# Attention with normalized q and k, then a mixture of depths: row transfers on another queue, a split first step and a split last store

## The chip, the cores and the metric

The kernel runs on one core of one Trainium2 chip. The core has five engines that run their own instruction streams: TensorE (PE; its weight loads stand as PEld), VectorE (DVE), ScalarE (ACT), GpSimd (POOL) and SyncE (SP), which here only issues transfers. They wait for each other through semaphores. The metric is the time on the device in microseconds. Its median over three runs is 543.24 us, with runs from 542.14 to 544.32. The profile is one further execution, whose span is 539.9 us.

## What is computed

The first half is attention over 8 batches, 12 heads, 448 positions and 64 values per head, in float32. Each row of q and k is divided by its root mean square. The second half sends 128 of the 448 tokens of each batch through two matrices.

```
q_n = q / sqrt(mean(q*q) + 1e-6) * g_q          # the same for k with g_k
attn = softmax(q_n @ k_n^T / sqrt(64))
x[b] = concatenation over the 12 heads of attn @ v          # (8, 448, 768)

scores = x @ w_gate
out = x
for each batch b:
    top = the 128 tokens with the highest scores
    ye  = relu(x[b, top] @ w1) @ w2             # 768 -> 1024 -> 768
    out[b, top] = x[b, top] + sigmoid(scores[b, top]) * ye
```

## The kernel before

The work is cut into 24 groups of 4 heads (3 groups to a batch), and each group into 7 units of 64 keys for each of the 4 heads. For a unit, TensorE makes scores, ScalarE their exponentials, TensorE the products with v, and VectorE adds up the exponentials. The softmax needs no maximum, because the normalized scores are bounded. Slots count the units, in order of the program: what is put in slot 20 is written into the program right after the units of about that number. An engine works through its own part of the program in order.

The inverse root mean squares are called rinv. There are two tiles of tokens for each group: tile 0 holds q (its rinv is 128 x 14 values), tile 1 holds k. The rinv of k enters as the scale of the exponential. The rinv of q has to be multiplied along the free axis of the transposed q. For groups 2 to 23 this goes by way of device memory: rows_out writes the values there as rows, rows_in reads them back spread over 64 partitions into bc, and scale_q multiplies. For groups 0 and 1, scale_q_early spreads them with TensorE.

```
class Loads:                      # in __init__: the first transfers
    nc.scalar.dma_start(out=self.gcol, in_=g2)
    ...
    nc.scalar.activation(out=warm, in_=neg_half, func=AF.Exp)
    self.load("tok", 0, 0)
    self.load("tok", 0, 1)
    self.load("qT", 0)
    # load() issues on SyncE: self.nc.sync.dma_start(out=t, in_=src)

...   # in fast(): identity, further loads, then the warm-up of TensorE
for _ in range(36):
    nc.tensor.transpose(out=ps[:, 0:128], in_=ident, identity=ident)

def squares(n, i):                # ScalarE
    t = get("tok", n, i)
    sq = norm_pool.tile([128, 2, NI, D], F32, name="sq")
    nc.scalar.activation(out=sq, in_=t, func=AF.Square, scale=scale)
    ...

def sum_squares(n, i, sq):        # VectorE, then GpSimd twice
    ss = sss.pop((n, i))
    nc.vector.tensor_reduce(out=ss, in_=sq, axis=AX.X, op=OP.add)      # L208
    nc.gpsimd.tensor_scalar_add(ss, ss, 1e-6)                          # L209
    rinv = norm_pool.tile([128, 2, NI], F32, name="rinv", bufs=8)
    nc.gpsimd.tensor_tensor(out=rinv..., in0=ss..., in1=neg_half..., op=OP.pow)   # L212

def rows_out(n):                  # GpSimd's queue, two transfers
    rows = dram_pool.tile([GH, S], F32, name="rows", bufs=3)
    rinv = rinvs.pop((n, 0))
    for c in range(2):
        nc.gpsimd.dma_start(                                           # L226
            out=rows[2 * c : 2 * c + 2].rearrange("h (p i) -> p h i", i=NI),
            in_=rinv[D * c : D * (c + 1)])

def rows_in(n):                   # SyncE's queue, two transfers (L238)
    ...
def scale_q(n):                   # VectorE (L247): qT = qT * gg * bc
    ...
def scale_q_early(n):             # TensorE (L259) spreads rinv; VectorE (L267) multiplies
    ...

# scores(u): TensorE L290, ScalarE's exponential p L299; values(u): TensorE L316
# add_probs(u): VectorE L333; sum_keys, invert_sums, to_tokens: L362, L377, L393

def mixture(b):                   # the two matrices for one batch
    ...                           # transposes L525; first matrix L544; relu into hT L553
    for a in range(2):
        cols = slice(DM // 2 * a, DM // 2 * (a + 1))                   # DM = 768
        ps = bank()
        for fc in range(NFC):                                          # NFC = 8
            nc.tensor.matmul(out=ps[:n, : DM // 2], lhsT=hT[:, fc, :n],
                             rhs=w2[:, fc, cols], ...)                 # L563
        nc.vector.scalar_tensor_tensor(out=xe[:n, cols], ...)          # L572
        if a == 1:
            nc.gpsimd.indirect_dma_start(                              # L581
                out=out.flatten_outer_dims(),
                out_offset=bass.IndirectOffsetOnAxis(ap=row[:n, :1], axis=0),
                in_=xe[:n, 0:DM], in_offset=None)

def prepare(n, slot):             # when the normalization of group n is written
    sq = {}
    for i in range(2):
        at(slot + 2 * i, lambda i=i: sq.setdefault(i, squares(n, i)))
        at(slot + 2 * i + 1, lambda i=i: sum_squares(n, i, sq.pop(i)))
    at(slot + 1, rows_out, n)
    at(slot + (8 if n > 5 else 6), rows_in, n)
```

In the schedule, s0 is the number of a group's first unit, and the normalization starts at slot s0 - 20 (s0 - 17 up to group 5), or at 0.

Of the kernel before, what the change touches and what calls it, by code (L numbers as in the profile page):

```python
# [10 lines left out]
F32 = mybir.dt.float32  # L11
I32 = mybir.dt.int32
AF = mybir.ActivationFunctionType
# [12 lines left out]
class Loads:  # L26


    def __init__(self, nc, pool, qT, kT, vp, tok, g2):
        self.nc, self.pool = nc, pool  # L30
        self.src = {"tok": tok, "qT": qT, "kT": kT, "v": vp}
        self.tiles = {}
        self.groups = tok.shape[1]
        self.gcol = pool.tile([128, 2], F32, name="gcol", bufs=1)
        nc.scalar.dma_start(out=self.gcol, in_=g2)
        neg_half = pool.tile([128, 1], F32, name="neg_half", bufs=1)
        nc.vector.memset(neg_half, -0.5)

        warm = pool.tile([128, 1], F32, name="warm", bufs=1)
        nc.scalar.activation(out=warm, in_=neg_half, func=AF.Exp)  # L40
        self.neg_half = neg_half
        self.load("tok", 0, 0)
        self.load("tok", 0, 1)
        self.load("qT", 0)

    def load(self, name, n, i=None):
        b, g = divmod(n, self.groups)
        src = self.src[name]
        if i is not None:
            src = src[b, g, :, i]  # L50
        elif name == "v":
            src = src[b, g]
        else:
            src = src[b, 2 * g : 2 * g + 2].rearrange("c p s -> p c s")
        pool = self.v_pool if name == "v" else self.pool
        bufs = {"tok": 6, "qT": 4, "kT": 3, "v": 3}[name]
        held = [key for key in self.tiles if key[0] == name]
        if len(held) == bufs:
            del self.tiles[held[0]]
        t = pool.tile(list(src.shape), F32, name=name, bufs=bufs)  # L60
        self.nc.sync.dma_start(out=t, in_=src)
        self.tiles[name, n, i] = t

    def get(self, name, n, i=None):
# [4 lines left out]
def fast(  # L69
# [26 lines left out]
    D = 64  # L96
# [36 lines left out]
        return ps_aux.tile(shape, F32, tag="aux", name=name)  # L133

    sss, rinvs, bcs = {}, {}, {}
    loads.v_pool = ctx.enter_context(tc.tile_pool(name="load_v", bufs=1))
    load, get, neg_half = loads.load, loads.get, loads.neg_half

# [59 lines left out]

    def squares(n, i):
        t = get("tok", n, i)  # L200
        sq = norm_pool.tile([128, 2, NI, D], F32, name="sq")
        nc.scalar.activation(out=sq, in_=t, func=AF.Square, scale=scale)  # L202
        sss[n, i] = norm_pool.tile([128, 2, NI], F32, name="ss", bufs=4)
        return sq

    def sum_squares(n, i, sq):
        ss = sss.pop((n, i))
        nc.vector.tensor_reduce(out=ss, in_=sq, axis=AX.X, op=OP.add)  # L208
        nc.gpsimd.tensor_scalar_add(ss, ss, 1e-6)  # L209
        rinv = norm_pool.tile([128, 2, NI], F32, name="rinv", bufs=8)  # L210
        flat = "p h i -> p (h i)"
        nc.gpsimd.tensor_tensor(  # L212
            out=rinv.rearrange(flat),
            in0=ss.rearrange(flat),
            in1=neg_half.to_broadcast([128, 2 * NI]),
            op=OP.pow,
        )
        rinvs[n, i] = rinv

    def rows_out(n):  # L220

        rows = dram_pool.tile([GH, S], F32, name="rows", bufs=3)
        rinv = rinvs.pop((n, 0))
        for c in range(2):

            nc.gpsimd.dma_start(  # L226
                out=rows[2 * c : 2 * c + 2].rearrange("h (p i) -> p h i", i=NI),
                in_=rinv[D * c : D * (c + 1)],
            )
        bcs[n] = rows  # L230

    def rows_in(n):

        rows = bcs[n]
        bc = norm_pool.tile([128, 2, S], F32, name="bc")
        for hh in range(2):
            src = rows.rearrange("(c hh) s -> hh c s", hh=2)[hh]
            nc.sync.dma_start(  # L238
                out=bc[D * hh : D * (hh + 1)],
                in_=dataclasses.replace(src, ap=[[0, D]] + [list(x) for x in src.ap]),  # L240
            )
        bcs[n] = bc
# [265 lines left out]
    def mixture(b):  # L508

        n = CAP  # L510
        xe = xes.pop(b)
        xeT = moe_pool.tile([128, NDC, 128], F32, name="xeT")

        def bank():

            if PER * now[0] >= units:
                return ps_sc.tile([128, 512], F32, tag="sc", name="sc")
            return ps_moe.tile([128, 512], F32, tag="moe", name="moe_ps")

        half = NDC // 2  # L520
        for a in range(2):
            ps = bank()
            for i in range(half):
                dc = half * a + i
                nc.tensor.transpose(  # L525
                    out=ps[:, 128 * i : 128 * i + n],
                    in_=xe[:n, 128 * dc : 128 * (dc + 1)],
                    identity=ident[:n, :n],
                )
            nc.scalar.copy(  # L530
                out=xeT[:, half * a : half * (a + 1), :n],
                in_=ps[:, : half * 128].rearrange("p (i t) -> p i t", t=128)[:, :, :n],
            )
            if a == 1:
                row = moe_pool.tile([128, 1], I32, name="row", bufs=2)
                nc.vector.tensor_copy(out=row[:n], in_=xe[:n, DM + 1 : DM + 2])
            yield

        hT = moe_pool.tile([128, NFC, 128], F32, name="hT")
        for f0 in range(0, NFC, 4):  # L540
            ps = bank()
            for i in range(4):
                for dc in range(NDC):
                    nc.tensor.matmul(  # L544
                        out=ps[:, 128 * i : 128 * i + n],
                        lhsT=w1[:, dc, 128 * (f0 + i) : 128 * (f0 + i + 1)],
                        rhs=xeT[:, dc, :n],
                        start=(dc == 0),
                        stop=(dc == NDC - 1),
                    )  # L550
                if i == 1:
                    yield
            nc.scalar.activation(  # L553
                out=hT[:, f0 : f0 + 4, :n],
                in_=ps.rearrange("p (i t) -> p i t", t=128)[:, :, :n],
                func=AF.Relu,
            )
            yield
        for a in range(2):
            cols = slice(DM // 2 * a, DM // 2 * (a + 1))  # L560
            ps = bank()
            for fc in range(NFC):
                nc.tensor.matmul(  # L563
                    out=ps[:n, : DM // 2],
                    lhsT=hT[:, fc, :n],
                    rhs=w2[:, fc, cols],
                    start=(fc == 0),
                    stop=(fc == NFC - 1),
                )
                if fc == NFC // 2 - 1:  # L570
                    yield
            nc.vector.scalar_tensor_tensor(  # L572
                out=xe[:n, cols],
                in0=ps[:n, : DM // 2],
                scalar=xe[:n, DM : DM + 1],
                in1=xe[:n, cols],
                op0=OP.mult,
                op1=OP.add,
            )
            if a == 1:  # L580
                nc.gpsimd.indirect_dma_start(  # L581
                    out=out.flatten_outer_dims(),
                    out_offset=bass.IndirectOffsetOnAxis(ap=row[:n, :1], axis=0),
                    in_=xe[:n, 0:DM],
                    in_offset=None,
                )
            yield
# [11 lines left out]
    def at(slot, fn, *args):  # L599
        todo.setdefault(slot, []).append(lambda: fn(*args))  # L600
# [14 lines left out]
    def prepare(n, slot):  # L615
        sq = {}
        for i in range(2):
            at(slot + 2 * i, lambda i=i: sq.setdefault(i, squares(n, i)))
            at(slot + 2 * i + 1, lambda i=i: sum_squares(n, i, sq.pop(i)))
        at(slot + 1, rows_out, n)  # L620
        at(slot + (8 if n > 5 else 6), rows_in, n)

    for n in range(1, n_groups):
        s0 = NI * n
# [1 line left out]
            at(max(s0 - 26, 4 * (n - 3)), load, "tok", n, 0)  # L626
            at(max(s0 - 26, 4 * (n - 3)), load, "tok", n, 1)
        if n > 1:
            first = max(s0 - (20 if n > 5 else 17), 0)
            prepare(n, first)  # L630
            at(max(s0 - 7, first + 10), scale_q, n)
            at(max(s0 - 13, 2), load, "qT", n)
            at(max(s0 - 11, 2), load, "kT", n)
            at(max(s0 - 11, 2), load, "v", n)
    for part in range(NDC + NFC):
        at(16 + 3 * part, load_w, part)
    at(7, lambda: nc.sync.dma_start(out=wg, in_=_bcast_row(moe_w_gate, CP)))
# [61 lines left out]

    for i in range(2):  # L700
        sum_squares(0, i, squares(0, i))
    sqs = [squares(1, i) for i in range(2)]
    scale_q_early(0)
    for i in range(2):
        sum_squares(1, i, sqs[i])
    load("tok", 2, 0)
    load("tok", 2, 1)
    task((0, 1), scale_q_early, 1)
# [570 lines left out]
```

## Time and profile before

| what | us |
|---|---|
| median of three runs | 543.24 |
| span of the profiled execution | 539.9 |
| TensorE busy | 513.1 |
| VectorE busy | 339.9 |
| ScalarE busy | 278.0 |
| GpSimd busy | 242.7 |

The profile is read from the busiest engine down. Busy time counts an instruction from its start to its end, and for TensorE the ends are modelled. A row of a group of instructions names the line, the engine, the operation and the tiles (out <- in), the count, the busy time with the mean in ns, and then the idle time of that engine just ahead of them with what ended it. A row of waits has the engine and line that waited, what it waited for, and the total in us, the number and the longest. L numbers are lines of the kernel before; they stand beside the code above. A q after an engine's name means its issuing part, for example SPq.

### The profile page before, as it was taken

The numbers are of one execution on the slowest core, as the hardware profiler recorded it, in microseconds if no ns is written. First come the engines' busy times: TensorE is split into PE (matmuls) and PEld (weight loads), VectorE is DVE, ScalarE is ACT, GpSimd is POOL, SyncE is SP. The second block draws the span as 40 slices with busy tenths as digits, with TensorE's granted clock in tenths as the row PEclk, the third lists the DMA queues.
The fourth block names the chain that finished last, engine by engine and source line by source line (L and its number), as shares of the span: only waits on it lengthen the run. The fifth ranks groups of instructions, "written<-read, shape, count | busy, mean of one in ns | idle before, by whom it ended". The sixth has DMA issues, their size and how long they took to land. (4 is left out here: it accounts for less than half of the span.)

```text
span 539.9 us, 16470 instructions
## 1 busy us (share of the span) xinstructions
PE 513.1 (95%) x7116; PEld 288.9 (54%) x7116; DVE 339.9 (63%) x644; ACT 278.0 (51%) x506; POOL 242.7 (45%) x193
## 2 busy tenths in 40 slices
PE   5999899999999999999999999999999999999991
PEld 5434344446644466546654466543764456568770
DVE  3767899788475776659557795668756384443000
ACT  3687786774535755546545755547564444311000
POOL 4785988657624276244734456336742103002000
PEclk9999999999999999999999999999999999999997
DMA  8957869999961497608826486604934032004100
GB/s 299 351 164 247 280 218 330 326 317 297 297 199 39 127 256 223 206 31 223 243 110 207 123 263 214 209 4 133 296 110 135 32 104 60 2 23 139 60 4 33
DMA packets 41605, 93.57 MB, mean 173 GB/s; under 512 B 6454, under 2 KB 24374, under 8 KB 41524
## 3 DMA queue, kind: packets, MB, share of 16 engines
q1 hardware_dynamic: 36772, 85.96, 50.6%
q0 software_dynamic: 4608, 6.47, 3.7%
q8 instruction: 58, 0.95, 0.7%
q14 instruction: 23, 0.19, 0.1%
q10 hardware_dynamic: 144, 0.00, 0.0%
HBM read 74.93 MB, written 25.35 MB: 186 GB/s over the span
## 5 line engine op out<-in xcount | busy, mean ns | idle before, releaser
L299 ACT ACTIVATE p<-sc,rinv 128x448 f32<-128x448 f32 x336 | 186.1, 639 | 109.5 <-PE sc L290 91.4
L316 PE MATMUL av<-p,v 64*32 64x448 f32 x2688 | 153.7, 537 | 0.0
L290 PE MATMUL sc<-qT,kT 64*32 64x448 f32 x2688 | 152.9, 540 | 0.3
L212 POOL TENSOR_TENSOR rinv<-ss,neg_half 128x14 f32<-128x14 f32 x48 | 138.6, 2888 | 4.0
L333 DVE TENSOR_TENSOR sum<-sum,p 128x896 f32<-128x896 f32 x113 | 122.5, 1084 | 9.2 <-ACT p L299 2.2
L316 PEld LDWEIGHTS av<-p,v 64*32 64x32 f32 x2688 | 58.2, 107 | 75.2 <-issue 70.8
L209 POOL TENSOR_SCALAR ss<-ss 128x14 f32<-128x14 f32 x48 | 23.0, 479 | 158.1 <-DVE ss L208 132.0
L290 PEld LDWEIGHTS sc<-qT,kT 64*32 64x32 f32 x2688 | 49.4, 106 | 70.8 <-issue 49.0
L544 PE MATMUL moe_ps<-xeT,w 128*128 128x128 f32 x576 | 69.5, 277 | 0.4 <-issue 0.4
L544 PEld LDWEIGHTS moe_ps<-xeT,w 128*128 128x128 f32 x576 | 66.2, 192 | 5.0 <-issue 5.0
L208 DVE TENSOR_REDUCE ss<-sq 128x14 f32<-128x896 f32 x48 | 51.4, 1077 | 27.6 <-ACT sq L202 24.2
L393 DVE TENSOR_TENSOR x<-x_ps,rden 112x512 f32<-112x512 f32 x48 | 32.9, 689 | 54.5 <-PE x_ps L391 50.3
L563 PE MATMUL moe_ps<-w,hT 128*128 128x384 f32 x176 | 61.2, 491 | 0.0
L487 POOL DMA_INDIRECT selected<-x,rank x32 | 36.4, 1138 | 35.0 <-DVE x L479 26.2
L202 ACT ACTIVATE sq<-tok 128x896 f32<-128x896 f32 x48 | 46.0, 963 | 7.2 <-DMA tok<-in_tok_dram 7.1
L581 POOL DMA_INDIRECT out_dram<-xe,row x8 | 10.8, 1348 | 79.6 <-DVE rden L379 47.5
L563 PEld LDWEIGHTS moe_ps<-w,hT 128*128 128x128 f32 x176 | 31.7, 190 | 21.8 <-issue 2.9
L417 DVE SCALAR_TENSOR_TENSOR prod<-x,wg 112x256 f32<-112x256 f32 x96 | 40.9, 426 | 3.0
L226 POOL DMA_DIRECT2D rows<-rinv x44 | 29.1, 662 | 6.6 <-POOL rinv L212 6.5
L391 PEld LDWEIGHTS x_ps<-ident,xT 128*112 128x112 f32 x192 | 21.0, 134 | 18.9 <-issue 12.7
L391 PE MATMUL x_ps<-ident,xT 128*112 128x128 f32 x192 | 29.1, 278 | 1.4 <-DVE x L393 1.4
L572 DVE SCALAR_TENSOR_TENSOR xe<-sc,xe 128x384 f32<-128x384 f32 x5 | 3.1, 618 | 41.0 <-PE sc L563 41.0
(66 smaller groups left out, 340.8 us busy)
## 6 DMA issues: line engine op xcount, KB each, us to landing
tok<-in_tok_dram SPq DMA_DIRECT2D x48, 448.0 KB
qT<-in_qT_dram SPq DMA_DIRECT2D x24, 448.0 KB
kT<-in_kT_dram SPq DMA_DIRECT2D x24, 448.0 KB
v<-in_vp_dram SPq DMA_DIRECT2D x24, 448.0 KB
out_dram<-x SPq DMA_DIRECT2D x8, 1344.0 KB
bc<-rows SPq DMA_DIRECT2D x44, 224.0 KB
xe<-selected SPq DMA_DIRECT2D x8, 385.0 KB
w<-in_moe_w_dram SPq DMA_DIRECT2D x6, 512.0 KB
```

Source lines behind the costliest of these rows:

```text
L202: nc.scalar.activation(out=sq, in_=t, func=AF.Square, scale=scale)
L208: nc.vector.tensor_reduce(out=ss, in_=sq, axis=AX.X, op=OP.add)
L212: nc.gpsimd.tensor_tensor(out=rinv.rearrange(flat), in0=ss.rearrange(flat), in1=neg_half.to_broadcast([128, 2 * NI]), op=OP.pow,)
L290: nc.tensor.matmul(out=scs[hh][o : o + 32, 0:S], lhsT=get("kT", n)[r, c, D * i + k0 : D * i + k0 + 32], rhs=get("qT", n)[r, c, :], start=True,
L299: nc.scalar.activation(out=p[:, hh], in_=scs[hh][:, 0:S], func=AF.Exp, scale=rinvs[n, 1][:, hh, i : i + 1],)
L316: nc.tensor.matmul(out=avs[n][c][o : o + 32, 0:S], lhsT=get("v", n)[r, hh, i, d0 : d0 + 32], rhs=probs[u][r, hh], start=(i == 0), stop=(i ...
L333: nc.vector.tensor_tensor(out=sums[n], in0=probs[u - 1] if i == 1 else sums[n], in1=probs[u], op=OP.add)
L391: nc.tensor.transpose(out=ps[:CP, j, :], in_=t[:, j, :], identity=ident)
L417: nc.vector.scalar_tensor_tensor(out=prod, in0=xs[b][:, j, cols], scalar=1.0, in1=wg[:, cols], op0=OP.mult, op1=OP.mult, accum_out=gates[b ...
L487: w = nc.gpsimd.indirect_dma_start(out=t[:, :], out_offset=bass.IndirectOffsetOnAxis(ap=rank[:, j : j + 1], axis=0), in_=x[:, j, :], in_of ...
L544: nc.tensor.matmul(out=ps[:, 128 * i : 128 * i + n], lhsT=w1[:, dc, 128 * (f0 + i) : 128 * (f0 + i + 1)], rhs=xeT[:, dc, :n], start=(dc == 0),
L563: nc.tensor.matmul(out=ps[:n, : DM // 2], lhsT=hT[:, fc, :n], rhs=w2[:, fc, cols], start=(fc == 0), stop=(fc == NFC - 1),)
```

## The change

It has five parts.

- The first tile of tokens is issued on ScalarE's queue, ahead of everything else there, instead of on SyncE's. It is meant to arrive sooner.
- For this first tile the squares and their sums are made in two halves, so that ScalarE and VectorE can overlap.
- The 1e-6 stands in a 65th column of two fixed tiles of squares, set once. The reduction adds it, and GpSimd's addition is gone.
- The rows of rinv are written by one transfer on SyncE's queue, later than before, instead of two on GpSimd's. Their layout in device memory is changed so that one transfer does, and the reads and the scaling of q are moved by one to three slots.
- For the last batch, the second matrix is worked in three parts of 256 columns instead of two of 384, and each part is stored by its own scatter as soon as it is ready. The store at the end is meant to be shorter.

```
-        self.load("tok", 0, 0)                      # after the warm exponential, on SyncE
+        self.load("tok", 0, 0, nc.scalar)           # ahead of gcol, on ScalarE

+    sqs = [const.tile([128, 2, NI, D + 1], F32, name=f"sq{i}") for i in range(2)]
+    for sq in sqs:
+        nc.vector.memset(sq[:, :, :, D], 1e-6)

     def squares(n, i):
-        sq = norm_pool.tile([128, 2, NI, D], F32, name="sq")
-        nc.scalar.activation(out=sq, in_=t, func=AF.Square, scale=scale)
+        sq = sqs[(2 * n + i) % 2]
+        for h in [slice(0, 1), slice(1, 2)] if (n, i) == (0, 0) else [slice(0, 2)]:
+            nc.scalar.activation(out=sq[:, h, :, 0:D], in_=t[:, h], func=AF.Square, scale=scale)

     def sum_squares(n, i, sq):
-        nc.vector.tensor_reduce(out=ss, in_=sq, axis=AX.X, op=OP.add)
-        nc.gpsimd.tensor_scalar_add(ss, ss, 1e-6)
+        for h in [slice(0, 1), slice(1, 2)] if (n, i) == (0, 0) else [slice(0, 2)]:
+            nc.vector.tensor_reduce(out=ss[:, h], in_=sq[:, h], axis=AX.X, op=OP.add)

     def rows_out(n):
-        rows = dram_pool.tile([GH, S], F32, name="rows", bufs=3)
-        rinv = rinvs.pop((n, 0))
-        for c in range(2):
-            nc.gpsimd.dma_start(
-                out=rows[2 * c : 2 * c + 2].rearrange("h (p i) -> p h i", i=NI),
-                in_=rinv[D * c : D * (c + 1)],
-            )
+        rows = dram_pool.tile([2, 2 * S], F32, name="rows", bufs=3)
+        nc.sync.dma_start(
+            out=rows.rearrange("h (p i) -> p h i", i=NI), in_=rinvs.pop((n, 0))
+        )
     def rows_in(n):
-            src = rows.rearrange("(c hh) s -> hh c s", hh=2)[hh]
+            src = rows[hh].rearrange("(c s) -> c s", c=2)

     # in prepare(n, slot)
-        at(slot + 1, rows_out, n)
-        at(slot + (8 if n > 5 else 6), rows_in, n)
+        at(slot + (7 if n > 2 else 6), rows_out, n)
+        at(slot + (10 if n > 5 else 9 if n > 2 else 8), rows_in, n)
     # in the schedule; the loads of qT, kT and v now stand ahead of prepare(n, first)
-            at(max(s0 - 7, first + 10), scale_q, n)
+            at(max(s0 - 6, first + 11), scale_q, n)

     # in mixture(b): parts_out is 3 for the last batch and 1 otherwise
-        for a in range(2):
-            cols = slice(DM // 2 * a, DM // 2 * (a + 1))
+        width = DM // max(2, parts_out)
+        for c0 in range(0, DM, width):
+            cols = slice(c0, c0 + width)
     ...
-            if a == 1:
+            if parts_out > 1 or c0 + width == DM:
+                part = slice(c0 if parts_out > 1 else 0, c0 + width)
                 nc.gpsimd.indirect_dma_start(
+                    out=out.flatten_outer_dims().rearrange("r (k c) -> (r k) c", k=parts_out),
     ...             # row holds 3 * token + part for part 0, 1, 2 of the last batch
```

More of the change, by code (lines that the diff above doesn't have):

```diff
@@ L41, in __init__, with load @@
         self.neg_half = neg_half
-        self.load("tok", 0, 0)
         self.load("tok", 0, 1)
         self.load("qT", 0)
-    def load(self, name, n, i=None):
+    def load(self, name, n, i=None, engine=None):
         b, g = divmod(n, self.groups)
@@ L60, in load @@
         t = pool.tile(list(src.shape), F32, name=name, bufs=bufs)
-        self.nc.sync.dma_start(out=t, in_=src)
+        (engine or self.nc.sync).dma_start(out=t, in_=src)
         self.tiles[name, n, i] = t
@@ L511, in mixture @@
         xe = xes.pop(b)
+        parts_out = 1 if b < B - 1 else 3
         xeT = moe_pool.tile([128, NDC, 128], F32, name="xeT")
@@ L534, in mixture @@
             if a == 1:
-                row = moe_pool.tile([128, 1], I32, name="row", bufs=2)
-                nc.vector.tensor_copy(out=row[:n], in_=xe[:n, DM + 1 : DM + 2])
+                row = moe_pool.tile([128, parts_out], I32, name="row", bufs=2)
+                for part in range(parts_out):
+                    nc.vector.tensor_scalar(
+                        out=row[:n, part : part + 1],
+                        in0=xe[:n, DM + 1 : DM + 2],
+                        scalar1=float(parts_out),
+                        scalar2=float(part),
+                        op0=OP.mult,
+                        op1=OP.add,
+                    )
             yield
@@ L563, in mixture @@
                 nc.tensor.matmul(
-                    out=ps[:n, : DM // 2],
+                    out=ps[:n, :width],
                     lhsT=hT[:, fc, :n],
@@ L573, in mixture @@
                 out=xe[:n, cols],
-                in0=ps[:n, : DM // 2],
+                in0=ps[:n, :width],
                 scalar=xe[:n, DM : DM + 1],
@@ L579, in mixture @@
             )
-            if a == 1:
+            if parts_out > 1 or c0 + width == DM:
+                part = slice(c0 if parts_out > 1 else 0, c0 + width)
                 nc.gpsimd.indirect_dma_start(
-                    out=out.flatten_outer_dims(),
-                    out_offset=bass.IndirectOffsetOnAxis(ap=row[:n, :1], axis=0),
-                    in_=xe[:n, 0:DM],
+                    out=out.flatten_outer_dims().rearrange("r (k c) -> (r k) c", k=parts_out),
+                    out_offset=bass.IndirectOffsetOnAxis(
+                        ap=row[:n, part.start * parts_out // DM :][:, :1], axis=0
+                    ),
+                    in_=xe[:n, part],
                     in_offset=None,
@@ L628, in fast @@
         if n > 1:
-            first = max(s0 - (20 if n > 5 else 17), 0)
-            prepare(n, first)
-            at(max(s0 - 7, first + 10), scale_q, n)
             at(max(s0 - 13, 2), load, "qT", n)
@@ L634, in fast @@
             at(max(s0 - 11, 2), load, "v", n)
+            first = max(s0 - (20 if n > 5 else 17), 0)
+            prepare(n, first)
+            at(max(s0 - 6, first + 11), scale_q, n)
     for part in range(NDC + NFC):
@@ L701, in fast @@
         sum_squares(0, i, squares(0, i))
-    sqs = [squares(1, i) for i in range(2)]
+    later = [squares(1, i) for i in range(2)]
     scale_q_early(0)
     for i in range(2):
-        sum_squares(1, i, sqs[i])
+        sum_squares(1, i, later[i])
     load("tok", 2, 0)
```

## The prediction

> **What bounds the kernel now.** I read the page first, then TensorE's own waits, then the timeline of the first 28 us and of the last 30 us, and last the waits of SyncE's queue. The page says who is busy, and what the parts that change cost in total:
>
> ```profile
> span 539.9 us, 16470 instructions
> ...
> PE 513.1 (95%) x7116; PEld 288.9 (54%) x7116; DVE 339.9 (63%) x644; ACT 278.0 (51%) x506; POOL 242.7 (45%) x193
> ...
> L212 POOL TENSOR_TENSOR rinv<-ss,neg_half 128x14 f32<-128x14 f32 x48 | 138.6, 2888 | 4.0
> ...
> L209 POOL TENSOR_SCALAR ss<-ss 128x14 f32<-128x14 f32 x48 | 23.0, 479 | 158.1 <-DVE ss L208 132.0
> ...
> L226 POOL DMA_DIRECT2D rows<-rinv x44 | 29.1, 662 | 6.6 <-POOL rinv L212 6.5
> ```
>
> TensorE is busy for 513.1 of 539.9 us, so 26.8 us of its idle time is all that a better schedule could win. It idles 5.3 us before its first instruction and 11.2 us after its last (539.9 - 528.7). That leaves 10.3 us for everything between. The waits of TensorE alone tell what those are:
>
> ```profile
> PE warm_ps L160 <- DVE gg L154: 5.3, 1, 5.3
> PE moe_ps L525 <- ACT xeT L530: 2.2, 3, 1.2
> PE den_ps L362 <- DVE x L393: 2.1, 5, 0.5
> ```
>
> No row there names rinv, rows, bc or a load. The middle waits are for the ScalarE and VectorE copies that surround the transposes. GpSimd, from which the change takes work, is 45% busy and nobody on TensorE waits for it.
>
> The timeline of the start (start us, duration us, engine, line, operation, and in brackets the idle time ahead):
>
> ```profile
> 5.26 6.42 PE L160 MATMUL warm_ps<-ident 128*128 128x128 f32 x36 [5.26 <-DVE gg L154]
> ...
> 5.35 2.03 ACT L202 ACTIVATE sq<-tok 128x896 f32<-128x896 f32 x2 [2.65 <-DMA tok<-in_tok_dram]
> ...
> 6.33 2.17 DVE L208 TENSOR_REDUCE ss<-sq 128x14 f32<-128x896 f32 x2 [1.16 <-ACT sq L202]
> ...
> 7.52 0.27 POOL L209 TENSOR_SCALAR ss<-ss 128x14 f32<-128x14 f32 x1 [2.35 <-DVE ss L208]
> ...
> 7.87 2.62 POOL L212 TENSOR_TENSOR rinv<-ss,neg_half 128x14 f32<-128x14 f32 x1
> ...
> 11.61 1.67 PE L259 MATMUL sc<-ident,rinv 64*64 64x64 f32 x56
> ...
> 15.18 4.54 ACT L299 ACTIVATE p<-sc,rinv 128x448 f32<-128x448 f32 x8 [2.74 <-PE sc L290]
> ```
>
> The reader is to compare two times. The first rinv is ready at 7.87 + 2.62 = 10.49 us. The 36 warm-up transposes, which stand ahead of its user in TensorE's program, hold TensorE until about 11.6 us. The spread of rinv over q (L259) starts at 11.61, directly behind them. The rinv chain thus has 1.1 us of slack already. The second rinv ends at 13.53 us and the first exponential, which reads it, starts at 15.18 us after waiting for scores: 1.6 us of slack.
>
> The tail: the timeline of the last 30 us, then two of the half-microsecond stretches (length, GpSimd busy, clock, share of the DMA engines, GB/s), then the instructions of the program's closing line (durations in ns min/median/max, first and last start):
>
> ```profile
> 518.23 10.49 PE L563 MATMUL sc<-w,hT 128*128 128x384 f32 x32
> 528.75 0.62 DVE L572 SCALAR_TENSOR_TENSOR xe<-sc,xe 128x384 f32<-128x384 f32 x1 [4.54 <-PE sc L563]
> 529.64 0.96 POOL L581 DMA_INDIRECT out_dram<-xe,row  x1 [21.29 <-DVE xe L572]
> ```
> ```profile
> 531.50:532.00 0.50, 0.00 (x0) 1.00 1.01 406
> 532.00:532.50 0.50, 0.00 (x0) 0.73 0.23 78
> ```
> ```profile
> L1206 POOLq DRAIN  x3: 40/107/7006, 532.1 to 539.6; - x3
> ```
>
> The rows have left by 532.5 us. Yet the span ends 7.4 us later, because a drain of GpSimd begins at 532.1 and lasts 7.0 us. It, and not the landing of the rows, is what ends last.
>
> [...] SyncE spends 0.36, 0.23 and 0.83 us on two weight rows and two token tiles before q is issued, and in 3.75 to 6.25 us the engines already carry about 400 GB/s. [...]
>
> **The change, part by part.**
>
> *First tokens from ScalarE's queue.* SyncE issues them at 1.48 us now; ScalarE can at 0.79, where it now issues gcol. That is 0.7 us sooner at best. The two token tiles then share the engines, so I take 0.4 us. ScalarE's table load (1.28 us from 1.20) slides by one issue, 0.4 us, and still ends at 2.9 us, before the tokens.
>
> *First squares in halves.* Square takes 0.95 us for 896 elements and the reduction 1.08. In halves the second half's square runs beside the first half's reduction: 0.5 + 0.55 + 0.55 = 1.6 us in place of 2.1, so 0.5 us.
>
> *1e-6 in a column.* The L209 addition goes: 0.27 us and its hop of 0.08, so 0.35 us per rinv at the start. Over the kernel, 23.0 us less on GpSimd. The reduction reads 910 elements in place of 896: 48 x 1.08 us x 14/896 = 0.8 us more on VectorE in all, which is 63% busy.
>
> Sum for the first rinv: 0.4 + 0.5 + 0.35 = 1.25 us sooner, at about 9.2. The second, behind one more addition, comes 1.6 us sooner. But TensorE is not free before 11.6 us, and the exponentials wait for scores, not rinv. On the end: **0 us**.
>
> *Rows from SyncE's queue.* GpSimd loses 44 issues, 29.1 us. SyncE gains 22, at some 0.6 us each (its bc issues have a median of 0.60), so 13 us over the kernel. The issue moves from 1 slot after the squares begin to 6 or 7, and the read back by 2. What counts is whether bc is in time for the scaling of q, and that for its scores. From the timelines I take four groups of heads (1 group is 7 units of work). For the third group the reads are issued at 28.8 us, q scaled at 34.3 and the first scores at 40.5; for the fourth 40.4, 46.5, 53.7; for the ninth 107.1, 120.4, 133.8; for the seventeenth 262.8, 289.2, 303.0. The smallest of these gaps are 5.5 us from read to scaling and 6.2 us from scaling to scores. Two slots are about 4 us early (7 units take 13 us from 40.5 to 53.7) and 5 to 6 us later, where the reads of the ninth and seventeenth lead by 13 and 26 us. So the early groups come near their limit, but q is scaled 1 slot later as well. I put 0 to 0.5 us on it. SyncE waits for rows already:
>
> ```profile
> SPq L405 <- DMA out_dram<-xe,row: 123.6, 6, 34.3
> ...
> SPq L238 <- DMA rows<-rinv: 57.1, 11, 8.7
> ```
>
> A SyncE queue that stands still for 123.6 us without making TensorE wait for any load has room for 22 more waits of 2 to 3 us. In exchange, VectorE and ScalarE meet other neighbours in the middle, and the 10.3 us of small TensorE waits can shift by about 1 us either way. I take **-0.3 us**.
>
> *Last rows in thirds.* 32 matmul instructions of 384 columns take 10.49 us, 328 ns each; 76 of 128 columns (L544 in the last batch) take 8.65 us, 114 ns each. The line through both is 7 ns + 0.836 ns per column, so 256 columns take 221 ns, and 48 of them 10.6 us: 0.1 us more. The last VectorE update falls from 0.62 us to about 0.43 (the 256-wide one of L417 has a mean of 426 ns): 0.2 us less. So the last scatter starts 0.1 us sooner. A third takes 3.5 us on TensorE[...], so even if each scatter waits for the one before, none is late. If the drain starts from the issue and lasts 7.0 us whatever is in flight, the landing counts for nothing: -0.1 us. [...] I take **-0.5 us**.
>
> Sum: 0 - 0.3 - 0.5 = -0.8 us; with a little for what the smaller load on GpSimd may free, -1.0 us: 543.24 - 1.0 = **542.2 us**.
>
> **Rivals.** *The start counts in full*: rinv is 1.25 to 1.6 us sooner and everything after slides. For it speaks that GpSimd's chain fills 7.5 to 13.5 us without a hole. Against it speaks that L259 follows the warm-up without a gap. It would give about 541.0 with the tail.
>
> *SyncE's queue becomes the bound*: the rows queue behind loads of 448 KB, the reads wait for them in order, and the next k and v loads wait behind the reads. For it speak the 57.1 us that the reads wait already, and that the rows leave a queue of their own. Against it speak the gaps above. It would add 2 to 8 us: 545 to 551.
>
> *The drain depends on GpSimd's transfers*: if it clears what all of them left, 44 of 84 fewer would shorten it by up to half, 3.5 us: 539. If three scatters close together lengthen it, 543.5. The trace has one such drain, so it can't tell.
>
> **Range and chances.** The runs before differ by 2.2 us, the middle can shift by 1 us, [...] the rivals lie at 539 to 541 and at 545. A range of 539.6 to 544.4 us should hold it 8 times in 10. Over 2% faster is below 532.4 us, 40% of all of TensorE's idle time: 0.01. Over 2% slower is above 554.1, which needs the SyncE rival at its worst: 0.02. Within 2%: 0.97.
>
> **What would show it.** Right: L259 starts at 11.6 us again while the first rinv ends near 9.2; TensorE's waits name neither bc nor rows; GpSimd is busy about 190 us; the last scatter starts within 0.2 us of the same distance from the last hT. Wrong: L259 before 11.3 us; a wait of VectorE's q scaling for bc beyond 2 us in total, or of TensorE for loads of k or v; a closing drain other than 7.0 us.

## The result, and the profile after

The changed kernel takes 550.95 us (median of four runs, 548.78 to 551.16), beside 543.0 for four runs of the kernel before. The ratio is 1.0135, 95% interval 1.0102 to 1.0168 (here and below it is not quite the quotient of the two medians): the changed kernel is slower. The predicted range ended at 544.4.

The page of the kernel after, in the rows that answer to those shown before:

```profile
span 547.0 us, 16425 instructions
...
PE 521.1 (95%) x7132; PEld 294.8 (54%) x7132; DVE 341.4 (62%) x650; ACT 279.0 (51%) x507; POOL 182.5 (33%) x103
...
L217 POOL TENSOR_TENSOR rinv<-ss,neg_half 128x14 f32<-128x14 f32 x48 | 131.0, 2734 | 239.7 <-DVE ss L214 196.3
```

GpSimd gives up 60 us, as planned, and this buys nothing by itself. TensorE is busy 8 us longer with hardly more instructions. The waits (total, times, longest, in us) show four rows that have grown. Before, their totals were 5.3, 0.6, 2.1 and 1.7 us, in the order shown:

```profile
PE warm_ps L164 <- DVE gg L158: 6.9, 1, 6.9
...
DVE qT L248 <- DMA bc<-rows: 5.7, 2, 3.0
...
PE den_ps L363 <- DVE x L394: 3.8, 5, 2.2
DVE prod L1233 <- DMA g<-in_g_k_dram: 3.4, 1, 3.4
```

Setting the start of the same TensorE work in the two traces side by side shows where the distance arises. After the start TensorE is 1.0 us behind, at 95 us 1.8, at 126 us 4.9, and then, mostly in steps near 205, 267 and 397 us, 12.1 us behind at the last hT (530.52 against 518.43). From there to the end the changed kernel needs 16.4 us in place of 21.5. That makes 12.1 - 5.1 = 7.0 us, the difference of the spans but for rounding. Four places are thus to be explained.

**Start.** The timeline (start us, duration us; idle time ahead in brackets):

```profile
4.32 0.21 DVE L1233 TENSOR_TENSOR prod<-g 1x64 f32<-1x64 f32 x1 [3.40 <-DMA g<-in_g_k_dram]
6.22 1.89 ACT L207 ACTIVATE sq<-tok 128x448 f32<-128x448 f32 x3 [3.04 <-DVEq L1245]
...
6.92 5.78 PE L164 MATMUL warm_ps<-ident 128*128 128x128 f32 x36 [6.92 <-DVE gg L158]
...
12.64 1.67 PE L260 MATMUL sc<-ident,rinv 64*64 64x64 f32 x56
```

VectorE multiplies the two weight rows (L1233, L1216 before) at 4.32 us; before, it did so at 2.60. A branch on the result follows, and every engine passes it (ScalarE waits 3.04 us for the branch's value, L1245). So the warm-up begins at 6.92 in place of 5.26, and the spread of rinv at 12.64 in place of 11.61. The trace's packets show why: the packet of 256 bytes of the second weight row is issued at 1.20 us in both kernels, but moves at 3.68 us in place of 2.09, when the 448 KB token tile on ScalarE's queue has all but passed. The first weight row, which moves at 1.71 us, ahead of the tile, is not held up. In the trace the tile moves as 128 packets of 3584 bytes, the first at 1.80 us and the last at 3.77, and between the first weight row and 3.46 us no data of SyncE's queue move. How the two queues take turns is not shown.

**Near 120 us.** SyncE's issues for the eighth group, first in the kernel before, then after:

```profile
96.92 1.23 SPq L238 DMA_DIRECT2D bc<-rows  x2
98.25 1.02 SPq L61 DMA_DIRECT2D tok<-in_tok_dram  x2
99.31 0.42 SPq L190 DMA_DIRECT2D w<-in_moe_w_dram  x1
99.79 0.54 SPq L61 DMA_DIRECT2D kT<-in_kT_dram  x1
100.67 0.33 SPq L61 DMA_DIRECT2D v<-in_vp_dram  x1
```
```profile
97.90 0.86 SPq L61 DMA_DIRECT2D tok<-in_tok_dram  x2
98.81 0.42 SPq L194 DMA_DIRECT2D w<-in_moe_w_dram  x1
99.28 0.42 SPq L61 DMA_DIRECT2D kT<-in_kT_dram  x1
99.80 0.41 SPq L61 DMA_DIRECT2D v<-in_vp_dram  x1
100.33 1.44 SPq L239 DMA_DIRECT2D bc<-rows  x2
```

The read of bc has gone from the head of this train to its tail. Ahead of it now stand two token tiles, k and v at 448 KB each and a weight part of 384 or 512 KB: at least 2176 KB. From 99 to 111 us the transfer engines are 98% busy or more and move 319 GB/s (the mean of six stretches of 2 us: 375, 289, 347, 361, 232, 307). An estimate from these is 2228e3 bytes / 319e3 per us = 7.0 us of waiting in line, and 1.4 more for bc itself: 8.4 of the 10.5 us measured from issue to use. In the trace the packets of SyncE's queue, told apart by their sizes, begin in the order of issue: the 256 of k (1792 bytes each) from 103.23 to 106.10 us, the 256 of v and bc (3584 bytes) from 104.85 to 109.77, and the first of the weight part issued behind bc (3072 bytes) at 107.73. So bc, issued at 100.33, releases the scaling of q only at 110.8. The timelines of VectorE and TensorE, and three stretches (length, busy us of PE, PEld, DVE, ACT, POOL; clock; DMA share; GB/s):

```profile
110.80 1.15 DVE L248 SCALAR_TENSOR_TENSOR qT<-qT,gg,bc 128x896 f32<-128x896 f32 x1 [2.70 <-DMA bc<-rows]
```
```profile
122.11 0.58 PE L363 MATMUL den_ps<-sum,pick_pair 128*32 128x224 f32 x8 [2.15 <-DVE x L394]
```
```profile
120.00:123.00 3.00, 0.89 (x11) 0.47 (x11) 2.82 (x7) 1.43 (x4) 1.68 (x1) 1.00 0.24 71
123.00:126.00 3.00, 3.00 (x28) 0.93 (x34) 2.87 (x10) 1.62 (x4) 0.00 (x0) 0.50 0.88 276
126.00:129.00 3.00, 3.00 (x72) 1.13 (x64) 2.97 (x5) 2.04 (x4) 2.15 (x1) 0.93 1.03 284
```

VectorE stands still for 2.7 us with the addition of the exponentials piled up behind, falls behind TensorE, and 11 us later TensorE waits 2.15 us for it (0.46 before). The wait puts TensorE 1.7 us further behind, and the half clock that follows 1.4. In that stretch TensorE is busy 0.89 of 3 us, and the next 3 us run at half clock: 28 matmuls where the following stretch has 72. In the kernel before the clock stays at 1.00 here, with 66 and 72 matmuls in the same two stretches. Half clock is granted from 122.99 to 126.40 us, 3.41 us long, and begins 0.9 us after the wait of 2.15 us ends. By what rule the clock is set is not shown.

**Near 205, 267 and 397 us.** TensorE waits for no semaphore here, yet issues slowly. Two stretches of 1 us of the kernel after, same columns:

```profile
206.00:207.00 1.00, 1.00 (x10) 0.28 (x8) 0.02 (x1) 0.00 (x0) 0.88 (x1) 1.00 0.85 154
207.00:208.00 1.00, 1.00 (x8) 0.21 (x7) 0.00 (x0) 0.00 (x0) 0.69 (x2) 1.00 0.72 119
```

Eight to ten matmuls (L291) in 1 us at full clock; from 201.90 us the same line makes 32 in 1.73 us. The kernel before has such stretches too, near 90, 138 to 141 and 449 us. The changed kernel has six: these three places (91, 141 to 144 and 461 us) and the three steps. All nine begin while GpSimd issues the four indirect transfers that collect a batch's chosen tokens (selected <- x, L487 before and L488 after; in one batch of the change from 203.4 to 208.3 us), which take some 5 us in 60. The change doesn't touch these transfers, and two of eight batches pass them at the full rate in the changed kernel, five in the kernel before. So the trace shows where the stretches lie, and not what they are.

**Tail.** The last scatter, and GpSimd's instructions on the program's closing line:

```profile
541.65 0.95 POOL L595 DMA_INDIRECT out_dram<-xe,row  x1 [2.47 <-DVE xe L585]
```
```profile
L1223 POOLq DRAIN  x3: 45/113/4248, 541.9 to 546.7; - x3
```

The closing drain lasts 4.2 us in place of 7.0, and the span ends 5.3 us after the last scatter starts, in place of 10.3.

### The profile page after: what moved, and what is told of

Read it like the earlier page. It is cut to its first block, busy times and chain, and to the rows that moved or that the text cites. A ratio compares the mean times of both kernels' runs of the same rounds, so it can differ in the third digit from the quotient of the medians.

```text
span 547.0 us, 16425 instructions
## 1 busy us (share of the span) xinstructions
PE 521.1 (95%) x7132; PEld 294.8 (54%) x7132; DVE 341.4 (62%) x650; ACT 279.0 (51%) x507; POOL 182.5 (33%) x103
## 4 chain that ended last, share of the span: by engine, by line
PE 84%; DVE 7%; DMA 4%; issue 2%; ACT 2%; SPq 0%; DVEq 0%; POOL 0%; POOLq 0%; ACTq 0%
PE sc L291 23%; PE av L317 21%; PE moe_ps L556 12%; PE moe_ps L576 11%; PE sc L576 4%; PE x_ps L392 4%; PE sc L556 3%; DMA bc<-rows 3%; DVE sum L334 2%; PE den_ps L363 2%; DVE x L394 2%; DVE ss L214 1%; PE warm_ps L164 1%; PE denT_ps L378 1%; ACT p L300 1%
## 5 line engine op out<-in xcount | busy, mean ns | idle before, releaser
L217 POOL TENSOR_TENSOR rinv<-ss,neg_half 128x14 f32<-128x14 f32 x48 | 131.0, 2734 | 239.7 <-DVE ss L214 196.3
L291 PE MATMUL sc<-qT,kT 64*32 64x448 f32 x2688 | 160.1, 545 | 1.1 <-issue 0.7
L317 PE MATMUL av<-p,v 64*32 64x448 f32 x2688 | 157.1, 537 | 0.0
L291 PEld LDWEIGHTS sc<-qT,kT 64*32 64x32 f32 x2688 | 51.4, 106 | 75.6 <-issue 50.4
L214 DVE TENSOR_REDUCE ss<-sq 128x14 f32<-128x910 f32 (+1 forms) x49 | 52.2, 1071 | 20.5 <-ACT sq L207 20.4
L207 ACT ACTIVATE sq<-tok 128x896 f32<-128x896 f32 (+1 forms) x49 | 46.1, 949 | 5.8 <-DVEq L1245 3.0
L488 POOL DMA_INDIRECT selected<-x,rank x32 | 33.5, 1045 | 34.7 <-DVE x L480 26.3
L334 DVE TENSOR_TENSOR sum<-p 128x896 f32<-128x896 f32 x24 | 25.7, 1072 | 8.7 <-ACT p L300 8.7
L248 DVE SCALAR_TENSOR_TENSOR qT<-qT,gg,bc 128x896 f32<-128x896 f32 x22 | 25.2, 1147 | 5.7 <-DMA bc<-rows 5.7
L585 DVE SCALAR_TENSOR_TENSOR xe<-sc,xe 128x384 f32<-128x384 f32 (+1 forms) x6 | 3.3, 551 | 40.6 <-PE sc L576 40.6
```

The source lines that it names most:

```text
L207: nc.scalar.activation(out=sq[:, h, :, 0:D], in_=t[:, h], func=AF.Square, scale=scale)
L214: nc.vector.tensor_reduce(out=ss[:, h], in_=sq[:, h], axis=AX.X, op=OP.add)
L217: nc.gpsimd.tensor_tensor(out=rinv.rearrange(flat), in0=ss.rearrange(flat), in1=neg_half.to_broadcast([128, 2 * NI]), op=OP.pow,)
L291: nc.tensor.matmul(out=scs[hh][o : o + 32, 0:S], lhsT=get("kT", n)[r, c, D * i + k0 : D * i + k0 + 32], rhs=get("qT", n)[r, c, :], start=True,
L317: nc.tensor.matmul(out=avs[n][c][o : o + 32, 0:S], lhsT=get("v", n)[r, hh, i, d0 : d0 + 32], rhs=probs[u][r, hh], start=(i == 0), stop=(i ...
L334: nc.vector.tensor_tensor(out=sums[n], in0=probs[u - 1] if i == 1 else sums[n], in1=probs[u], op=OP.add)
```

## The experiments

They ran on three other chips, where the kernel before takes 534.4 to 534.8 us; each ratio is to the kernel before on the same chip. Unless it is said otherwise, there were 20 runs of each changed version.

### Each part alone

*Rows on SyncE's queue, with the later slots.* The kernel before with only this:

```
-            nc.gpsimd.dma_start(out=rows[2 * c : 2 * c + 2]..., in_=rinv[D * c : D * (c + 1)])
+        nc.sync.dma_start(out=rows..., in_=rinvs.pop((n, 0)))
-        at(slot + 1, rows_out, n);  at(slot + (8 if n > 5 else 6), rows_in, n)
+        at(slot + (7 if n > 2 else 6), rows_out, n)
+        at(slot + (10 if n > 5 else 9 if n > 2 else 8), rows_in, n)     # q, k, v loads ahead of prepare
```

> Rows on SyncE's queue with the moved slots, alone. Theory (late bc): the read of the rows lands late behind the loads on SyncE's queue, VectorE stands in front of the scaling of q, TensorE idles over 2 us near 120 us and loses its clock; the lag before the last batch is 8 to 11 us, and with the old closing drain the time is 550 to 554. Rival (drain follows GpSimd's transfers): the closing drain falls from 7.0 to about 4.2 us here, so the time is 546 to 550. Rival (the start makes it all): no change, 542 to 544.

Measured: 536.49 us, ratio 1.0034 (1.0021 to 1.0046). The timeline of VectorE has the late bc again:

```profile
80.54 1.15 DVE L243 SCALAR_TENSOR_TENSOR qT<-qT,gg,bc 128x896 f32<-128x896 f32 x1 [2.86 <-DMA bc<-rows]
109.28 1.15 DVE L243 SCALAR_TENSOR_TENSOR qT<-qT,gg,bc 128x896 f32<-128x896 f32 x1 [4.08 <-DMA bc<-rows]
```

TensorE's longest wait for x is 3.8 us, the clock is at half from 120.94 to 124.35 us, and from the last hT to the end it takes 17.9 us in place of 21.5. The closing drain, before 7.0 us long, is among GpSimd's instructions on the closing line:

```profile
L1203 POOLq DRAIN  x3: 40/107/3418, 528.8 to 532.8; - x3
```

So this part alone brings both the loss near 120 us (4.4 us behind, set beside the run with the column alone) and most of the gain at the end (3.6 us).

*First tokens on ScalarE's queue, squares in halves.*

```
+        self.load("tok", 0, 0, nc.scalar)      # ahead of gcol
-        self.load("tok", 0, 0)
+        for h in [slice(0, 1), slice(1, 2)] if (n, i) == (0, 0) else [slice(0, 2)]:   # squares, sums
```

> First tokens on ScalarE's queue and halves, alone. Theory (late branch): the two weight rows that decide the branch land behind the tokens, the branch opens 1.7 us later, the first spread of rinv starts at about 12.6 instead of 11.6 us, and the time is 543.5 to 545. Rival (chain of rinv counts, as the change meant): 541.5 to 542.5.

Measured: 536.68 us, ratio 1.0031 (1.0018 to 1.0044), or 1.7 us slower. The weight rows are multiplied at 4.21 us, the warm-up begins at 6.82, and the tail is that of before (21.5 us). The size is taken from the times, since one trace doesn't give it: between the runs with the thirds and the column alone, which share the old start, the first exponentials lie 1.3 us apart (15.65 and 14.32), and the full clock is granted at 11.1 and at 8.3 us.

*Last rows in thirds.* `parts_out = 1 if b < B - 1 else 3`, with the loop and scatter of the change.

> Last batch in thirds, alone. Theory (the closing drain depends on the last scatter or what is in flight): from the last hT to the end 15.9 us instead of 20.9, and the time is 537 to 539. Rival (the drain depends on how many transfers GpSimd had issued, the rows above all): still 20.5 us or more, 542 to 543.5.

Measured: 535.0 us, ratio 1.0006 (0.9992 to 1.002). The drain lasts 7.2 us and the tail 21.6. While the rows are on GpSimd's queue, the thirds give nothing.

*Column of 1e-6.* `sqs` with a 65th column, without the addition on GpSimd.

> 1e-6 in a column, alone: GpSimd loses 23 us, VectorE gains under 1 us, and nobody on the path waits for GpSimd, so 541.5 to 544 whatever the theory. If it is over 546, the rearrangement of the small waits in the middle is by itself enough to cost what the change costs.

Measured: 534.34 us, ratio 0.999 (0.9976 to 1.0004). The interval holds 1: GpSimd's 23 us were waited for by nobody.

### The whole again, and the rows part split

*The whole change again*, on a second and on a third chip.

> The whole change again, beside the kernel before on the chip of this call, because the slow stretches of TensorE at 205, 267 and 397 us were seen only on the chip of the first comparison. If the loss there is of the change's own three places (start about +1.7 us, a late bc about +5 us, drain and thirds about -5 us), the ratio here is 1.001 to 1.006 and no such stretches appear. If the stretches belong to the changed program, they appear here too and the ratio is near the first one, 1.0135 (7 us more).

Measured: 536.01 us, ratio 1.0027 (1.0016 to 1.0039).

> The whole change a third time, as control for this call: ratio 1.002 to 1.006 if this chip behaves as the last one, about 1.013 with slow stretches of TensorE near 205, 267 and 397 us if it behaves as the first.

Measured: 536.0 us, ratio 1.0022 (1.0012 to 1.0033). Neither trace has a slow stretch near 205, 267 or 397 us. The late bc is in both (7.6 and 7.0 us of waiting), and so are 3.4 us of half clock (from 122.5 and 125.1 us) and the short drain (4.25 us). So the three explained places make the change 0.2 to 0.3% slower, and the slow stretches, seen on the first chip alone, go with the rest.

*Rows on SyncE's queue in the old slots.* Only the rows_out and rows_in edits of the change; `at(...)` as before.

> Only the rows go by SyncE's queue, in the slots of the kernel before. Theory (the later slots make bc late: a read issued two slots later meets loads in a full queue): the wait of the q scaling for bc goes back to under 1 us in total, the clock drop near 122 us disappears, and the drain stays near 3.4 us, so about 3 us faster than before (ratio 0.993 to 0.996). Rival (the queue itself makes it late: a row write that waits for rinv holds everything behind it on SyncE): SyncE waits for GpSimd's rinv by tens of us, bc or k and v loads are late as before, ratio 1.002 or more.

Measured: 535.54 us, ratio 1.0019 (1.0005 to 1.0034). The drain lasts 3.4 us, the mean granted clock is 0.995 (0.994 with the later slots), and TensorE waits for x no longer than 0.5 us (3.8 with the later slots). But bc is late all the same: 12.1 us of waiting in 4 places. SyncE's waits name the cause:

```profile
SPq L223 <- POOL rinv L212: 182.4, 19, 20.3
```

Written one slot after the squares, the row transfer waits in SyncE's program for GpSimd's rinv, and every later load with it: q of the third group is issued at 24.7 us, where the kernel before issued it at 12.8. Here the rival was right. The later slots of the change are there for a reason.

*Later slots alone*, with the rows on GpSimd's queue.

> Only the slots move (rows written 5 to 6 slots later, read 2 later, q loads ahead of the preparation, q scaled 1 later); the rows stay on GpSimd's queue. Theory (late slots make bc late): the q scaling waits for bc by 3 to 7 us in total, a clock drop near 120 us, drain 7.0 us, about 4 to 5 us slower than before (ratio 1.008 to 1.010). Rival (the queue makes it late): no wait for bc above 1 us, ratio 0.999 to 1.001.

Measured: 545.81 us (four runs), ratio 1.0197 (1.015 to 1.0243). More than expected:

```profile
DVE qT L247 <- DMA bc<-rows: 17.7, 3, 8.2
```

The rows of the third group leave at 33.8 us; with the same slots on SyncE's queue they leave at 24.0. The reads wait 67.1 us for rows, where they waited 57.1 in the kernel before. The mean granted clock is 0.982 in the profiled run, where the runs of the kernel before on this chip have 0.990 to 0.994. With the late slots the ratio is 1.0034 on SyncE's queue (1.0019 with the old ones) and 1.0197 on GpSimd's.

*Rows on SyncE's queue in the old slots, with the column and the thirds.*

> Rows by SyncE's queue in the slots of before, the column of 1e-6 and the last rows in thirds; the start is that of before. If the parts add up: short drain about -3.5 us, thirds about -1.5 us more because the drain no longer hides them, column -0.3: 5 us faster than before (ratio 0.988 to 0.993). If the rows on SyncE's queue cost in the middle whatever the slot: ratio 0.997 or more, with a wait for bc or for a load.

Measured: 533.46 us, ratio 0.9984 (0.9967 to 1.0001). The tail takes 16.4 us, so 5 us are won there, but the time shows 1, and that is not clear of the noise. SyncE waits 193.4 us for rinv, and VectorE 8.5 us for bc. The profiled run was the fastest of 20 (529.56; the others reach up to 536.6), so its trace hides most of what the middle costs.

### Reads ahead of the loads

*The whole change, with the reads of bc ahead of k and v again:*

```
-        at(slot + (7 if n > 2 else 6), rows_out, n)
-        at(slot + (10 if n > 5 else 9 if n > 2 else 8), rows_in, n)
+        at(slot + (7 if n > 5 else 5), rows_out, n)
+        at(slot + (8 if n > 5 else 6), rows_in, n)
             # and prepare(n, first), scale_q ahead of the loads of q, k and v
```

> The whole change, but the read of the rows stands ahead of the k and v loads of its group again (2 or 3 slots earlier), with the write at most 1 slot ahead of it. Theory (the read is late because it stands behind 2.2 MB of token, weight, k and v loads in SyncE's queue): q scaling waits for bc under 2 us in total, no drop of the clock near 122 us, 4 to 5 us faster than the whole change, so a ratio to before of 0.993 to 0.996. Rival (the rows are late because SyncE's queue reaches the write late): the waits for bc stay above 5 us and the ratio above 1.000.

Measured: 530.51 us (four runs), ratio 0.9922 (0.9906 to 0.9939). No wait for bc is left, the mean granted clock is 0.998 in the profiled run (0.994 for the whole change on this chip), and the kernel is 5.5 us faster than the whole change beside it (536.0). Only the start still lags: TensorE waits 7.0 us for its first work, 1.8 more than in the next run.

*The same with the first tokens on SyncE's queue* (halves kept):

```
-        self.load("tok", 0, 0, nc.scalar)
+        self.load("tok", 0, 0)                 # where it was before
```

> The same, and the first tokens from SyncE's queue as before (the first squares stay in halves). Theory (the token tile on ScalarE's queue delays the two weight rows, and with them the branch and the warm-up): first transposes at 5.2 us in place of 6.9, and 1.5 to 2 us faster than the run with the reads ahead: ratio to before 0.989 to 0.993. Rival (the start is hidden by the clock's ramp): same as that run.

Measured: 528.41 us (four runs), ratio 0.9894 (0.987 to 0.9918), 2.1 us less again. It beats both kernels. The order of issue, and TensorE's waits at the start and in the middle:

```profile
95.92 1.09 SPq L239 DMA_DIRECT2D bc<-rows  x2
97.10 1.01 SPq L61 DMA_DIRECT2D tok<-in_tok_dram  x2
98.16 0.42 SPq L194 DMA_DIRECT2D w<-in_moe_w_dram  x1
98.64 0.60 SPq L61 DMA_DIRECT2D kT<-in_kT_dram  x1
```
```profile
PE warm_ps L164 <- DVE gg L158: 5.2, 1, 5.2
...
PE den_ps L363 <- DVE x L394: 2.1, 5, 0.5
```

Both wait rows have gone back to their values of before: the longest wait for x is 0.5 us, where it was 2.2. Beside the trace with the column alone, the tail is 5.1 us shorter, and TensorE wins 2.1 us at one place near 105 us. There, with the column alone, ScalarE's squares wait 3.6 us for a token tile and TensorE 1.0 us for the exponentials that stand behind them; here the squares wait 1.6 us and TensorE not at all. No run isolates this second gain.

*The same, but every second group's rows by GpSimd's queue:*

```
+        if n % 2:   # two transfers of 64 partitions, nc.gpsimd.dma_start
+        else:       # nc.sync.dma_start, as in the change
```

> The same again, but every second group's rows are written by GpSimd's queue in two issues as in the kernel before (22 issues in place of 44 before and 0 in the change). If GpSimd's closing drain grows with what its queue has carried: a drain halfway between 4.25 and 7.1 us, 5.2 to 6.2. If any such rows bring it: 7.0. If it depends on what is still in flight at the end: 4.25 again. The time follows the drain: 1 to 3 us more than with all rows on SyncE.

Measured: 531.53 us (four runs), ratio 0.9938 (0.9921 to 0.9955), 3.1 us more than with all rows on SyncE's queue. The closing drain, without such rows and with half of them:

```profile
L1223 POOLq DRAIN  x3: 45/113/4252, 520.4 to 525.2; - x3
```
```profile
L1227 POOLq DRAIN  x3: 40/113/6039, 523.5 to 530.1; - x3
```

The last of these rows are written at 407 us and read at 410, more than 100 us before the end, so nothing of theirs is in flight. Half the rows bring 1.8 us of drain; in the trace the rest of the loss lies mostly near 106 us, where TensorE waits 1.4 us for exponentials behind squares that wait 3.9 us for a token tile. With the last rows in thirds the drain lasts 4.25 us with no row transfers on GpSimd's queue, 6.0 with 22 and 7.2 with 44. Whether the number of transfers, their packets or their bytes count is not separated.

## Why the prediction was wrong

- **Middle, "-0.3 us": the failed step.** It rested on "A SyncE queue that stands still for 123.6 us without making TensorE wait for any load has room for 22 more waits of 2 to 3 us." The 22 writes are not what hurt: with the reads ahead, all of them go by SyncE's queue, with 47 us of waits for rinv and 69 for rows, and the time falls. What failed is that lateness was counted from the issue, by slots, and not from what stands in the queue at that issue. Two slots were "about 4 us early ... and 5 to 6 us later"; they moved the read behind 2.2 MB, 7 us by the estimate above. The four groups chosen also missed the two in which bc came late. From read to scaling, the sixth group had 6.0 us in the kernel before and takes 8.7 in the change, 3.0 of it waiting; the eighth had 7.5 (96.9 to 104.4 us) and takes 10.5, 2.7 of it waiting. Only the second wait reached TensorE with any size. In place of -0.3 us the term is +4.4 to +4.7 us in the traces of the other chips (3.1 on the first), and +5.5 us in time between the whole change and the run with the reads ahead. That is close to the middle of the rival "SyncE's queue becomes the bound" (2 to 8 us), which was given too little weight.
- **Start, "0 us".** Right: a shorter rinv chain wins nothing. In the change the first rinv isn't even sooner (10.70 us, put at 9.2; 10.49 before), because the branch holds the squares. With the first tokens back on SyncE's queue it ends at 9.74, and the spread of rinv still starts only as the warm-up ends, at 11.00. Wrong: sharing the engines was charged to the token tiles alone ("so I take 0.4 us"). The second weight row shared them too (it moved at 3.68 us in place of 2.09), and a branch for all engines hangs on it. That is +1.7 us alone, and 2.1 us when taken back.
- **Tail, "-0.5 us".** TensorE's 10.6 us for 48 matmuls of 256 columns came out at 10.53 and the last update of 0.43 at 0.48. The -0.5 us was the author's estimate; no trace then showed a scatter of a third. The drain was mis-sized: 7.0 was taken as fixed. Taking the rows off GpSimd's queue gives -3.6 us, the thirds -1.5 more (17.9 to 16.4), and without the first the thirds give nothing. For the rows the rival had the size right ("up to half, 3.5 us"); that the drain "clears what all of them left" is not shown.
- **Column.** Nobody waits for GpSimd: right. GpSimd was put at 190 us busy and measured 182.5; most of the difference is that its powers (L217) took 131.0 us in place of 138.6.
- **The sum.** On the two chips of the repeats the three terms, +1.7, +4.4 to +4.7 and -5.1, give 1.0 to 1.3 us; 1.2 to 1.6 were measured. On the first chip the trace has 1.0 us at the start, 0.8 more by 95 us, 3.1 near 120 us, 7.2 after 126 us and -5.1 in the tail. The 7.2 us are nearly all slow stretches. They were in no step, and most of the miss on that chip is theirs.

**What stays open.** Why the slow stretches exist on the first chip and not on three others, where the same indirect transfers pass at the full rate, and why the change has more of them. An instruction fetch precedes most of them by 0 to 3 us, but there are 58 fetches, one in 9.4 us, so this says little. No run here shows what the stretches are. The versions with the reads ahead were not measured on the first chip, so whether they are faster there is not shown.

## What to carry to other kernels

Before moving a small transfer that someone waits for, list what stands ahead of it in its queue and turn the bytes into time (here 2176 KB at the measured 319 GB/s, an estimate of 7.0 us). A slot in the program is not a time of arrival. And at the start of a kernel, ask what each small transfer gates before sending a large one beside it (here 256 bytes moved at 3.68 us in place of 2.09, beside 448 KB).

## What was not expected of the hardware

- GpSimd's closing drain with the last rows in thirds: 7.2 us with all 44 row transfers on its queue, 6.0 with 22, 4.25 with none. With a single last scatter: 7.0 with 44 and 3.4 with none. It begins 0.2 us after the last third starts, but 2.4 to 2.6 us after a single last scatter, and 2.5 us after the last third with all 44; why is open. From the start of the last scatter to the end of the span it takes, in thirds, 10.5, 7.1 and 5.3 us with 44, 22 and none, and with a single scatter 10.3 and 6.7.
- Soon after a wait of TensorE of 2.15 us, in the whole change, the clock was at half for 3.41 us, and after one of 3.8, with the rows part alone, for 3.41 us too. In the kernel before, where TensorE's longest wait after the start is 1.4 us, it stayed at full from 9.99 to 532.23 us.
- Written from SyncE's queue, the rows are 5632 packets of 28 bytes; from GpSimd's they were 704 of 224. The two fastest versions write them so, too.
